# One output transfer for a tile with rows of two batches, and a store issued by ScalarE

## The chip, the cores and the metric

The kernel runs on one core of one Trainium2 chip. The metric is the device time of one execution in microseconds; a kernel's time is the median of several executions. A core has a matrix engine (TensorE, "PE" in the profile), VectorE (DVE), ScalarE (ACT), GpSimd (POOL), SyncE (SP, which here issues nearly all transfers), and 16 DMA engines that move the data between the chip's memory (DRAM) and the core's on-chip memory (SBUF, 128 partitions).

## The reference

Attention with a few extra "beacon" keys, and behind it a gated feed-forward layer:

```python
B, H, S, Nb, D = (8, 8, 576, 16, 64)
k_all = np.concatenate([beacon_k, k], axis=2)      # v_all likewise
scores = scale * np.matmul(q, k_all.transpose(0, 1, 3, 2))
scores = np.where(causal, -1000000000.0, scores)   # beacon keys are always seen
a = np.exp(scores - scores.max(-1, keepdims=True))
a /= a.sum(-1, keepdims=True) + 1e-09
x = np.matmul(a, v_all).transpose(0, 2, 1, 3).reshape(4608, 512)
out = (np.maximum(x @ w_gate, 0.0) * (x @ w_val)) @ w_out    # d_ff = 1536
```

The result has 4608 rows (8 batches of 576) of 512 float32.

## The kernel before, in words

The work is a list of tasks. Each task has the engines that may run it, a cost, the tasks it depends on, the buffers it holds and a priority. A planner (`Plan.order`) goes through them once on the host: it always takes the task that can begin first by its own estimates (then the one with the lowest priority number), and so writes one order of instructions for each engine. On the chip each engine works through its own list in that order and waits with semaphores. A transfer is a task of the queue "DMA", which is SyncE's list; its cost has two parts, the time to issue and the time on the wire.

For every batch, q, k and v are loaded into staging tiles `st` (lines 534, 614, 615, 617 and others), cast on GpSimd (line 500 into `h`, line 456 for v), turned by TensorE against the identity (line 511) and copied to their places. Scores are matmuls of lines 675 to 683, the exponential is line 709 on ScalarE, the division by the sum line 730 on GpSimd. The scaled weights `pb` are transposed by DMA (line 776) for all batches but the first, and line 786 multiplies them with v. The result lands transposed in `xT`.

The feed-forward layer works on 512 of a batch's 576 rows at a time (`REG` = 512): `hidden` makes the gate and value products (line 853), the ReLU (857) and their product `hT` (861). `project` then multiplies 128 rows of `hT` with `w_out` in three groups of four matmuls (line 873), copies the result from the accumulator into an output tile `osb` (`copy`, line 452 on ScalarE or 454 on VectorE) and stores it (line 885). There are four `osb` tiles, each 128 rows of 512 float32.

The last 64 rows of each batch are left over. They are gathered from four batches at a time, so that `hidden` sees 256 rows, and `project` sees two tiles of 128 rows, each with 64 rows of one batch and 64 rows of the next. Those two blocks of a tile lie 576 rows apart in the output, and the kernel stores them with one transfer for each. This happens twice: for batches 0 to 3 in the middle of the run, for batches 4 to 7 at its very end. The very last tile (`last` is true) is projected in two halves of 256 columns (`LAST_PARTS` = 2), so that the first half can be copied and stored while the second is still being multiplied.

The store's priority (`OUT` = -1300) puts it ahead of the loads that could begin at the same moment. A buffer is given back once all its users are done, which is the `users` count of `Hold`.

Of the kernel before, what the change touches and what calls it, by code (L numbers as in the profile page):

```python
# [55 lines left out]
OUT = -1300.0  # L56
# [93 lines left out]
class Plan:  # L150
# [7 lines left out]
    def add(self, engines, cost, run, deps=(), holds=(), prio=0.0, lag=None, part=0, lazy=0.0, after=0.0, move=0.0):  # L158
        t = Task(engines if isinstance(engines, tuple) else (engines,), cost, run, deps, holds, prio, lag, part, lazy, move)
        t.ready = after  # L160
        for d in t.deps:
            d.users.append(t)
        self.tasks.append(t)
        return t
# [112 lines left out]
def kernel(  # L277
# [12 lines left out]
    nc = tc.nc  # L290
    B, H, S, D = q.shape
# [4 lines left out]
    P = 128  # L296
# [54 lines left out]
    osb_s = outs  # L351
# [7 lines left out]
    f_s, v_ps, first_ps = Share(banks, F_MOST), Share(banks, V_MOST), Share(banks, FIRST_MOST)  # L359
# [3 lines left out]
    add = plan.add  # L363


    def c_dve(n):
        return 0.07 + 0.00104 * n
# [7 lines left out]
    def c_act(n):  # L375
        return 0.06 + 0.00083 * n
# [4 lines left out]
    def c_pe(n):  # L381
        return 0.002 + n / 2400.0
# [67 lines left out]
    def copy(e, dst, src):  # L450
        if e == "ACT":
            nc.scalar.copy(dst, src)  # L452
        elif e == "DVE":
            nc.vector.tensor_copy(dst, src)  # L454
        else:
            nc.gpsimd.tensor_scalar(dst, src, 1.0, 1.0, ALU.mult, ALU.mult)
# [408 lines left out]
    def project(t0, rows, here, hT, prio, last):  # L865
        w = DM // LAST_PARTS if last else DM
        for n0 in range(0, DM, w):
            ps, osb = Hold(f_s, 4), Hold(osb_s, 1 + len(rows))
            prev = None
            for part in range(3):  # L870
                def outp(_, part=part, ps=ps, n0=n0):
                    for nf in range(4 * part, 4 * part + 4):
                        nc.tensor.matmul(ps.tile[:, :w], hT[nf].tile[:, t0:t0 + P], wo_r[:, nf, n0:n0 + w],  # L873
                                         start=(nf == 0), stop=(nf == NF - 1))

                need = [prev, weight_in["o", part]]
                for hid in here:
                    need += hid[4 * part:4 * part + 4] + (hid[:11] if part == 0 else [])
                prev = add("PE", 4 * c_pe(w), outp, need, (ps,) + tuple(hT[4 * part:4 * part + 4]),
                           prio + 0.3 + 0.01 * part + 0.001 * (n0 > 0) - (0.5 if part else 0))  # L880
            ev = add(("ACT", "DVE"), {"ACT": c_act(w), "DVE": c_dve(w)}, lambda x, ps=ps, osb=osb: copy(
                x.engine, osb.tile[:, :w], ps.tile[:, :w]), (prev,), (ps, osb), -1000 + prio)
            at = 0
            for r0, n in rows:
                add("DMA", (0.4, 0.78 * n / P), lambda _, osb=osb, r0=r0, n=n, at=at, n0=n0: nc.sync.dma_start(
                    out[r0:r0 + n, n0:n0 + w], osb.tile[at:at + n, :w]), (ev,), (osb,), prio + OUT)
                at += n


    T0 = 10.0  # L890
# [15 lines left out]
    REG = S // MT * MT  # L906
    for b in range(B):
        hT = [Hold(hid_s, len(CUTS.get(b, ())) + 1 + REG // P) for _ in range(NF)]
        cuts = [0, *CUTS.get(b, ()), REG]
        prio = 1000 + 10.0 * b  # L910
        here = []
        for a, z in zip(cuts, cuts[1:]):
            here.append(hidden(lambda ki, a=a, z=z, b=b: xT[:, ki, b * S + a:b * S + z], z - a, a, done(b, a, z), hT, prio))
            for t0 in range(a // P * P, z // P * P, P):
                project(t0, [(b * S + t0, P)], [x for x, c0, c1 in zip(here, cuts, cuts[1:]) if c0 < t0 + P and c1 > t0],
                        hT, prio, False)
            prio += 2.0
    ends = xT.rearrange("p k (b s) -> p k b s", s=S)
    for i in range(2):
        b0, b1 = i * B // 2, (i + 1) * B // 2  # L920
        w = (b1 - b0) * (S - REG)
        prio = 1000 + 10.0 * b1 - 5.0
        hT = [Hold(hid_s, 1 + w // P + (LAST_PARTS - 1) * i) for _ in range(NF)]
        deps = [x for b in range(b0, b1) for x in done(b, REG, S)]
        hid = hidden(lambda ki, b0=b0, b1=b1: ends[:, ki, b0:b1, REG:], w, 0, deps, hT, prio)
        for t0 in range(0, w, P):
            b = b0 + t0 // (S - REG)
            project(t0, [(x * S + REG, S - REG) for x in (b, b + 1)], [hid], hT, prio, i == 1 and t0 + P == w)
# [37 lines left out]
```

## Time and profile before

| | |
|---|---|
| median of 3 runs | 411.87 us (411.68 to 412.15) |
| profiled execution | 410.77 us, of which the span is 408.7 us |
| TensorE busy | 394.9 us, 97% of the span |
| mean granted TensorE clock | 0.995 |
| output stores | 32 of 256 KB, 6 of 128 KB, 4 of 64 KB, all issued by SyncE at line 885 |
| median time from issue to landing | 2.4, 2.9 and 2.0 us for these three sizes |
| share of the chain that ended last | PE 87%, DMA 4%, POOL 3% |

An engine's row gives its busy time; the issuing of a transfer is not counted as busy, but has its own rows under "SPq". "Landing" is the moment at which a transfer's completion has arrived. A DMA share of 1 means that all 16 DMA engines have packets under way; overlapping packets can carry it over 1.

### The profile page before, as it was taken

The page shows a single profiled execution, that of the slowest core. Times are in us where ns is not written, and L with a number is a line of the kernel's source. Part 1 is how long each engine was busy: PE and PEld are TensorE (multiplying, and loading weights), DVE is VectorE, ACT ScalarE, POOL GpSimd, SP SyncE. Part 2 cuts the span into 40 slices and gives each one's busy share as a digit, 9 for nine tenths or more (in the row PEclk, how much of TensorE's full clock was granted, in tenths as well). Part 3 has the DMA queues.
Part 4 walks back from the last instruction along what each step waited for, and adds up shares of the span by engine and source line. Part 5 has one row for each costly group of instructions (what it writes and reads, how often), then busy time and mean ns, then how long its engine had stood idle before and what let it go on. Part 6 is the DMA issues. An engine that isn't in the chain of part 4 may idle for free.

```text
span 408.7 us, 10385 instructions
## 1 busy us (share of the span) xinstructions
PE 394.9 (97%) x3292; PEld 248.0 (61%) x3326; DVE 312.5 (76%) x1160; ACT 289.0 (71%) x958; POOL 234.5 (57%) x435
## 2 busy tenths in 40 slices
PE   8899999999999999999999999999999999999993
PEld 6667867587766868545557754555545544444482
DVE  7999899868999988889968988999877433244241
ACT  5998799769988987887977999978868133033030
POOL 5899697548985859487693877857818000000000
PEclk9999999999999999999999999999999999999997
DMA  8999999799899989999899999999492740200112
GB/s 201 194 236 211 211 174 159 143 267 239 193 218 179 235 182 232 192 223 220 193 213 217 225 196 218 199 182 243 108 199 53 169 71 0 95 9 2 53 51 51
DMA packets 172615, 68.02 MB, mean 166 GB/s; under 512 B 146832, under 2 KB 168080, under 8 KB 172560
## 3 DMA queue, kind: packets, MB, share of 16 engines
q1 hardware_dynamic: 167808, 62.64, 74.4%
q0 software_dynamic: 4752, 4.72, 7.2%
q8 instruction: 26, 0.43, 0.5%
q14 instruction: 29, 0.24, 0.2%
HBM read 38.27 MB, written 9.44 MB: 117 GB/s over the span
## 4 chain that ended last, share of the span: by engine, by line
PE 87%; DMA 4%; POOL 3%; DVE 2%; issue 1%; SPq 1%; ACT 1%; POOLq 0%; DVEq 0%; ACTq 0%
PE f L853 44%; PE f L873 23%; PE f L683 7%; PE f L786 6%; PE f L511 4%; DMA st<-in_q_dram 3%; PE f L675 2%; POOL xT L730 1%; DMA st<-in_v_dram 1%; PE f L815 1%; DVE f L698 1%; PE f L765 1%; PE f L678 1%; POOL h L500 1%; SPq L534 0%
## 5 line engine op out<-in xcount | busy, mean ns | idle before, releaser
L730 POOL TENSOR_SCALAR pb<-pb,small 128x448 bf16<-128x448 bf16 (+8 forms) x224 | 122.2, 560 | 56.1 <-DVE small L723 49.7
L709 ACT ACTIVATE pb<-f,small 128x64 bf16<-128x64 f32 (+7 forms) x256 | 131.8, 531 | 8.3 <-DVE small L698 3.4
L857 ACT ACTIVATE g<-f 128x512 f32<-128x512 f32 (+3 forms) x156 | 71.9, 475 | 66.5 <-PE f L853 54.0
L698 DVE CUSTOM_DVE_ANT_0 f<-f,mask 128x128 f32<-128x128 f32 (+7 forms) x256 | 112.2, 475 | 5.3 <-PE f L683 4.2
L853 PE MATMUL f<-xT,wv_r 128*128 128x512 bf16 (+3 forms) x618 | 110.6, 313 | 0.3
L853 PE MATMUL f<-xT,wg_r 128*128 128x512 bf16 (+3 forms) x616 | 109.2, 313 | 0.5
L861 DVE TENSOR_TENSOR hT<-g,f 128x512 bf16<-128x512 f32 (+3 forms) x156 | 79.9, 520 | 38.6 <-PE f L853 34.6
L873 PE MATMUL f<-wo_r,hT 128*128 128x512 bf16 (+1 forms) x425 | 100.8, 373 | 1.1 <-issue 0.2
L853 PEld LDWEIGHTS <-wg_r 128*128 128x128 bf16 x624 | 59.7, 98 | 32.0 <-issue 0.3
L853 PEld LDWEIGHTS <-wv_r 128*128 128x128 bf16 x624 | 58.8, 98 | 33.3 <-issue 0.7
L873 PEld LDWEIGHTS <-hT 128*128 128x128 bf16 x444 | 41.8, 98 | 40.7
L709 ACT ACTIVATION_READ_ACCUMULATOR pb<-f,small 128x1 f32 x256 | 55.9, 218 | 0.0
L683 PE MATMUL f<-kT,diag 128*128 128x128 bf16 (+7 forms) x256 | 46.0, 286 | 0.0
L698 DVE DVE_READ_ACCUMULATOR2_ANT small<- 128x1 f32 x296 | 41.2, 139 | 0.2
L500 POOL TENSOR_SCALAR h<-st 128x512 bf16<-128x512 f32 x62 | 37.8, 619 | 5.2 <-DMA st<-in_q_dram 1.8
L454 DVE COPY osb<-f 128x512 f32<-128x512 f32 (+1 forms) x24 | 16.3, 679 | 25.9 <-PE f L873 25.7
L511 PE MATMUL f<-ident,h 128*128 128x128 bf16 (+2 forms) x320 | 28.4, 216 | 3.5 <-POOL h L500 3.5
L730 POOL TENSOR_SCALAR xT<-xT,small 128x64 bf16<-128x64 bf16 (+2 forms) x64 | 27.2, 442 | 6.8 <-PE f L853 5.5
L454 DVE CAST diag<-f 64x512 bf16<-64x512 f32 (+2 forms) x54 | 28.7, 537 | 2.8 <-ACT diag L452 1.4
L511 PEld LDWEIGHTS <-h 128*128 128x128 bf16 (+2 forms) x320 | 21.0, 98 | 14.4 <-POOL h L500 5.8
L709 ACT ACTIVATE xT<-f,small 128x64 bf16<-128x64 f32 (+4 forms) x64 | 27.4, 448 | 2.6 <-issue 1.3
L695 DVE TENSOR_REDUCE small<-f 128x1 f32<-128x512 f32 x40 | 27.2, 679 | 1.9 <-PE f L675 1.0
(68 smaller groups left out, 367.6 us busy)
## 6 DMA issues: line engine op xcount, KB each, us to landing
st<-in_q_dram SPq DMA_DIRECT2D x32, 256.0 KB, 4.4
st<-in_k_dram SPq DMA_DIRECT2D x32, 256.0 KB, 4.6
out_dram<-osb SPq DMA_DIRECT2D x32, 256.0 KB, 2.4
st<-in_v_dram SPq DMA_DIRECT2D x24, 256.0 KB, 5.2
st<-in_v_dram SPq DMA_DIRECT2D x8, 224.0 KB, 4.5
wg_r<-in_moe_w_gate_dram POOLq DMA_DIRECT2D x3, 512.0 KB, 10.5
wv_r<-in_moe_w_val_dram POOLq DMA_DIRECT2D x3, 512.0 KB, 10.6
wo_r<-in_moe_w_out_dram POOLq DMA_DIRECT2D x3, 512.0 KB, 10.8
```

The costliest lines, as they stand in the source:

```text
L454: nc.vector.tensor_copy(dst, src)
L500: (nc.gpsimd if x.engine == "POOL" else nc.vector).tensor_scalar(to, of, by, 1.0, ALU.mult, ALU.mult)
L511: nc.tensor.matmul(to, h16.tile[:rows, a * P:(a + 1) * P], ident[:rows, :rows], start=True, stop=True)
L683: nc.tensor.matmul(view(i), t.diag.tile[:, p, j * P:j * P + P], kT[:, p, :n], start=True, stop=True)
L695: nc.vector.tensor_reduce(out=to, in_=view(i), axis=AX.X, op=ALU.min)
L698: nc.vector.tensor_tensor_reduce(out=view(i), in0=view(i), in1=msk, scale=1.0, scalar=small["t"][:, 0:1] if name in "EF" else 3.0e38, op0= ...
L709: nc.scalar.activation(ph.tile.rearrange("p a n -> p (a n)")[:, a:a + n], view(i), AF.Exp, bias=small["t"][:, low:low + 1], scale=-1.0, ac ...
L730: (nc.gpsimd if x.engine == "POOL" else nc.vector).tensor_scalar(one, one, small["t"][:, 8 + i:9 + i], 1.0, ALU.mult, ALU.mult)
L853: nc.tensor.matmul(to, w_r[:, ki, nf * P:(nf + 1) * P], x, start=(ki == 0), stop=(ki == KM - 1))
L857: r = add("ACT", c_act(w), lambda _, psg=psg, g=g: nc.scalar.activation(g.tile[:, :w], psg.tile[:, :w], AF.Relu), (a,), (psg, g), -1000 + ...
L861: hid.append(add("DVE", c_dve(w), lambda _, psv=psv, g=g, nf=nf: nc.vector.tensor_mul(hT[nf].tile[:, c0:c0 + w], g.tile[:, :w], psv.tile[: ...
L873: nc.tensor.matmul(ps.tile[:, :w], hT[nf].tile[:, t0:t0 + P], wo_r[:, nf, n0:n0 + w], start=(nf == 0), stop=(nf == NF - 1))
```

## The change

The blocks of rows of a tile are no longer stored one by one. For a tile of one batch the transfer is the same as before. For a tile with rows of two batches, the output is viewed as batch by row by column, and one transfer goes from the 128 partitions of `osb` to 2 batches x 64 rows (`REG:` to the end of the batch) x `w` columns. The output tile is held by two users, the copy and the store. For the first half of the very last tile, the copy is tied to ScalarE, and the store is a task of ScalarE with a cost of 0.6 us at the copy's priority: ScalarE issues it, not SyncE. All other stores stay with SyncE. The planner's cost of a store is 0.4 us to issue and 0.78 us on the wire; before, each block had 0.4 us and its share of 0.78.

```diff
     def project(t0, rows, here, hT, prio, last):
         w = DM // LAST_PARTS if last else DM
         for n0 in range(0, DM, w):
-            ps, osb = Hold(f_s, 4), Hold(osb_s, 1 + len(rows))
+            ps, osb = Hold(f_s, 4), Hold(osb_s, 2)
...
             ev = add(("ACT", "DVE"), {"ACT": c_act(w), "DVE": c_dve(w)}, lambda x, ps=ps, osb=osb: copy(
                 x.engine, osb.tile[:, :w], ps.tile[:, :w]), (prev,), (ps, osb), -1000 + prio)
-            at = 0
-            for r0, n in rows:
-                add("DMA", (0.4, 0.78 * n / P), lambda _, osb=osb, r0=r0, n=n, at=at, n0=n0: nc.sync.dma_start(
-                    out[r0:r0 + n, n0:n0 + w], osb.tile[at:at + n, :w]), (ev,), (osb,), prio + OUT)
-                at += n
+            if last and n0 == 0:
+                ev.engines, ev.cost = ("ACT",), {"ACT": c_act(w)}
+            to = out[rows[0][0]:rows[0][0] + P, n0:n0 + w] if len(rows) == 1 else out.rearrange("(b s) d -> b s d", s=S)[
+                rows[0][0] // S:rows[0][0] // S + len(rows), REG:, n0:n0 + w]
+            if last and n0 == 0:
+                add("ACT", 0.6, lambda _, osb=osb, to=to: nc.scalar.dma_start(to, osb.tile[:, :w]), (ev,), (osb,), -1000 + prio)
+                continue
+            add("DMA", (0.4, 0.78), lambda _, osb=osb, to=to: nc.sync.dma_start(to, osb.tile[:, :w]), (ev,), (osb,), prio + OUT)
```

## The prediction

> **What bounds the kernel now.** I read the page first (busy times and slices), then the chain of work that ended last for the final 30 us, then the timeline and the transfers of the output for the last 7 us, and last the stretch around 240 us where the first stores of two-batch tiles stand.
>
> The busy times and the table of 10 us stretches say that TensorE sets the pace: it has 97% of the span, and 9.89 to 9.95 us of each 10 us around the middle stores.
>
> ```profile
> PE 394.9 (97%) x3292; PEld 248.0 (61%) x3326; DVE 312.5 (76%) x1160; ACT 289.0 (71%) x958; POOL 234.5 (57%) x435
> ...
> 240.00:250.00 10.00, 9.89 (x53) 4.93 (x53) 9.23 (x40) 9.61 (x34) 6.01 (x12) 1.00 0.93 184
> ```
>
> The reader is to see that only two places are open to this change: the tail after the last matmul, and any stall that it puts into TensorE's row of work. The chain and the instruction queue of SyncE show the tail (start, length in us, what):
>
> ```profile
> 397.40 4.96 PE f L873 x34
> 402.36 0.02 issue
> 402.38 0.42 DVE osb L454
> ...
> 402.23 3.70 SPq L885 DMA_DIRECT2D out_dram<-osb  x6
> ...
> L885 SPq DMA_DIRECT2D out_dram<-osb x2: 546/566/587, 404.7 to 405.3; - x2
> ...
> DMA to landing us min/median/max: 2.0/2.0/2.1
> ...
> L961 SPq EVENT_SEMAPHORE  x11: 17/28/28, 406.0 to 408.7; - x11
> ```
>
> The last matmul ends at 402.34, the last copy at 402.80, but SyncE hands out six stores one behind the other from 402.23 to 405.93. The last of them, issued at about 405.34, lands 2.0 to 2.1 us later, near 407.4, and the closing waits end the span at 408.7. So 402.8 to 407.4 is spent on stores alone, some 2.5 us of it because the last store is sixth in the queue.
>
> What a store costs the 16 DMA engines is in two tables of stretches (the last two columns: busy share of the engines, GB/s). The first is a whole 128-row store behind TensorE's work, the others are the 64-row stores of the tail:
>
> ```profile
> 383.00:383.90 0.90, 0.90 (x5) 0.39 (x4) 0.07 (x1) 0.00 (x0) 0.00 (x0) 1.00 0.79 291
> ...
> 403.30:404.00 0.70, 0.00 (x0) 0.00 (x0) 0.00 (x0) 0.00 (x0) 0.00 (x0) 1.00 0.85 178
> 404.00:404.60 0.60, 0.00 (x0) 0.00 (x0) 0.00 (x0) 0.00 (x0) 0.00 (x0) 0.80 0.98 212
> ```
>
> A whole store moves 256 KB in 0.9 us at 291 GB/s with 0.79 of 16 engines busy: 291 / 16 / 0.79 = 23.0 GB/s for one busy engine. A store from 64 of the 128 partitions has the same 2 KB rows but only 178 to 212 GB/s, with the engines as busy.
>
> Last, the middle, in SyncE's queue, then GpSimd's and TensorE's rows for what the loads behind the stores feed:
>
> ```profile
> 239.29 3.52 SPq L885 DMA_DIRECT2D out_dram<-osb  x4
> 242.87 0.58 SPq L614 DMA_DIRECT2D st<-in_beacon_v_dram  x1
> 243.49 0.44 SPq L615 DMA_DIRECT2D st<-in_v_dram  x1
> 243.97 0.56 SPq L534 DMA_DIRECT2D st<-in_q_dram  x1
> ...
> DMA to landing us min/median/max: 3.8/3.8/3.8
> ...
> 248.59 0.62 POOL L500 TENSOR_SCALAR h<-st 128x512 bf16<-128x512 f32 x1
> ...
> 251.11 0.39 PE L511 MATMUL f<-ident,h 128*128 128x128 bf16 x4
> ```
>
> Four 64-row stores go out ahead of the loads of the next batch. The q load issued at 243.97 lands 3.8 us later at 247.8, is cast at 248.59 to 249.21 and turned by TensorE at 251.11: slack of 0.8 us before the cast and 1.9 us behind it, 2.7 us in all.
>
> **The change part by part.** (1) Ten 64-row stores become five 128-row ones: two in place of four at 239 us, three in place of six at the tail. (2) The store of the last tile's first half moves from SyncE to ScalarE's queue. (3) The copy of that half is tied to ScalarE, which made it already (0.37 us from 401.94): nothing. (4) The planner sees one issue of 0.4 us in place of two and the same 0.78 us of transfer, and the output buffer counts two users. Its loads may be handed out up to 0.4 us earlier; what follows could come in another order. A gain is bounded by TensorE's idle time in those stretches, 0.05 to 0.16 us in each 10 us, about 1 us to the end; a loss I bound by the same 1 us. I take 0.
>
> Issue time. At the tail SyncE issues two stores in place of six; the whole stores above took 0.33 us to issue, the 64-row ones 0.51 to 0.59. The last copy ends at 402.80 and SyncE is free by then (402.23 + 0.59), so the last store is issued at 402.85 instead of 405.34: 2.5 us sooner. ScalarE issues its store at about 402.35, right behind its copy, with only the closing drain queued behind it. The trace shows no issue by ScalarE; by SyncE's rows it is 0.33 to 1.59 us (the longest in the middle, with its queue full), beside the last copy, so 0 on the path.
>
> How the rows of a store are dealt to the engines decides the rest. Each hardware-queue load or store of the trace has a count of rows as its outermost count, 128, 112, 80, 64, 48 or 16; 16 divides them all, and each transfer ends with 16 small completion writes in the packet records. The q and k loads have a count of two as well, but inside the 128. The new stores are the first with a two outside: their DRAM side is 2 batches of 64 rows, 576 rows apart, while the SBUF side is 128 partitions. The trace cannot show whether they are dealt by rows (16 engines) or by the outermost count (2 engines), so both ends stand.
>
> The cheap end, 16 engines: whole stores as in the 291 GB/s row, 0.9 us for the first and 0.45 us for each half, landing at about 405.1 (402.85 + 2.0 to 2.4). 405.1 - 407.4 = -2.3 us, and the middle gains nothing, as TensorE has no wait there.
>
> The dear end, 2 engines: 2 x 23.0 = 46 GB/s. The tail's 512 KB take 11.4 us. The first data come 0.9 us after an issue (a whole store issued at 382.24 began to move near 383.1), so 403.1 + 11.4 = 414.5, and 0.4 us to the landing, as now: 414.9 against 407.4 is +7.5 us. All three stores use the same two engines, so ScalarE's queue saves nothing. In the middle the two stores also hold 512 KB: from 240.2 to 251.6 on these two engines, where the data of the four stores now end near 244.2 (fourth landing 244.6, less 0.4). Every load behind them has a sixteenth of its rows on each of these engines and so ends 7.4 us late; 2.7 us are slack, then GpSimd's cast waits, and TensorE stands still for 4.7 us at line 511. Bounds here: 0, if buffers and the order of work absorb it; and the whole 7.4 us plus as much again, if the 128x512 transposes by DMA (4.3 us to issue at 245.28) queue up too, 14 us.
>
> I take 2 engines. The nearest rows are the 64-row stores: they show that work is cut by position beforehand and not shared out, since engines freed of half the partitions brought no speed; and one cut by the outermost count fits every transfer of the trace without exception. The sum: -0 for issue (hidden behind the data), +7.5 at the tail, +4.7 in the middle: +12.2 us. The profiled execution took 410.77 us (span 408.7 and 2.07 around it): 423.0. It lies 1.1 us under the median of 411.87, so for the median: 424.1.
>
> The Trainium skill, page "DMA: Bandwidth & Descriptors", section "Rules for kernel authors", states that an outermost dimension of size c below 16 confines the whole transfer to at most c engines; by it the sum is the dear end, and no run here shows it yet. It speaks against this change; the same section also advises one transfer of 128 partitions in place of two from disjoint halves, which speaks for it, and by which alone the sum would be the cheap end.
>
> **The rivals.** (a) Dealt by rows, the cheap end: 411.87 - 2.3 = 409.6 us, faster. For it: the SBUF side still counts 128 and whole stores run at 291 GB/s. Against: the two blocks are not one run in DRAM. The point from which it decides: data must end by 407.0 to break even, 3.9 us for 512 KB, so 134 GB/s or 5.8 engines; with six or more engines the change gains, with fewer it loses. (b) Two engines, but the middle hidden: 411.87 + 7.5 = 419.4 us. For it: transposes by DMA land 9 us before use in that stretch (landing at 252, used at 261.5). Against: the 2.7 us of slack at the q load. (c) Two engines at the 64-row rate of some 12 GB/s each: twice the data times, +18.9 at the tail and 18.8 - 2.7 = 16 in the middle, about 447 us. Against: 24 GB/s in total is far under the 178 GB/s that half the partitions gave. (d) No difference: six engines, or a new queue's start cost on ScalarE that eats the 2.3 us: 411.9.
>
> **How the numbers follow.** Chances: forecast 0.62, (a) 0.13, (b) 0.20, (c) 0.02, (d) 0.03. A difference of 0.2% (0.8 us) is about what a measurement of this kernel can tell. Slower is 0.62 + 0.20 + 0.02 = 0.84, same 0.03, faster 0.13. Predicted 424 us. The range takes the forecast and (b) with their bounds: the low end is (b) with the three last stores on three different pairs of engines, where the longest, 256 KB at 46 GB/s, takes 5.7 us and lands at 409.2, +1.8, so 414; the high end is the forecast with the middle at 14 us, 433. It leaves out (a), (c) and (d), 0.18. The forecast's own range is 420 to 433.
>
> **What would show it.** In the profile after: three output stores at the tail, the last issued near 402.85 plus what the middle cost, landing some 12 us later, with a DMA share near 0.12 and about 46 GB/s in those stretches. In the middle: two stores landing 6 and 12 us after their issue, loads behind them 7 us late, and TensorE waiting 4 to 5 us for the casts of line 500. Landings 2.0 to 2.4 us after the issue and 291 GB/s would mean (a), and the prediction would be wrong in its step on dealing; an unbroken TensorE near 250 us would mean (b).

## The result, and the profile after

The changed kernel takes 426.72 us (median of 4 runs, 426.35 to 428.14) against 412.01 us before (4 runs of the same session): 3.6% slower, ratio 1.0364 with a 95% interval of 1.0339 to 1.0389. The forecast was 424 us, range 414 to 433. The profiled execution of the changed kernel took 428.14 us, of which the span is 426.4; it began about 1.5 us later than the one of before (the first matmul of line 853 stands at 34.8 us and not at 33.3, long ahead of anything that was changed), so positions below are compared with that in mind. This start moves between 32.6 and 35.2 us over all the profiled runs of this study.

The page of the changed kernel, its first lines and the slices of the DMA engines:

```profile
span 426.4 us, 10384 instructions
...
PE 397.8 (93%) x3290; PEld 249.0 (58%) x3326; DVE 312.1 (73%) x1156; ACT 288.3 (68%) x962; POOL 233.5 (55%) x435
...
DMA  8999998999999999999999749989866400101101
...
q10 hardware_dynamic: 130, 0.13, 0.1%
```

TensorE's share falls from 97% to 93%, while its busy time hardly moves (394.9 to 397.8 us): the time is waiting. The new queue q10 is ScalarE's; it carries 128 rows and two completion writes, 130 packets, where a transfer over 16 engines ends with 16.

The tail, first the chain that ended last, then the timeline, and then a table of stretches (last columns: granted TensorE clock, share of the 16 DMA engines, GB/s):

```profile
406.84 4.96 PE f L873 x34
411.80 0.02 issue
411.82 0.42 DVE osb L454
```

```profile
411.66 1.20 SPq L890 DMA_DIRECT2D out_dram<-osb  x2
411.78 1.30 ACTq L888 DMA_DIRECT2D out_dram<-osb  x1
```

```profile
413.50:414.50 1.00, 0.00 (x0) 0.00 (x0) 0.00 (x0) 0.00 (x0) 0.00 (x0) 1.00 0.13 20
414.50:416.50 2.00, 0.00 (x0) 0.00 (x0) 0.00 (x0) 0.00 (x0) 0.00 (x0) 0.70 0.13 39
416.50:418.50 2.00, 0.00 (x0) 0.00 (x0) 0.00 (x0) 0.00 (x0) 0.00 (x0) 0.50 0.13 51
```

The issues did what the change says: the last store is handed out at 412.35, 0.6 us after the last matmul, and not 3.0 us after it. Yet from the last matmul to the end of the span pass 14.6 us (411.8 to 426.4), where 6.4 us passed before. The share of 0.13 is two engines of 16 (2 / 16 = 0.125). They begin slowly, with 20 GB/s, and move about 50 GB/s from 416.5 us on.

The middle, in TensorE's timeline and waits, and GpSimd's timeline:

```profile
251.20 0.57 PE L683 MATMUL f<-kT,diag 128*128 128x448 bf16 x2
257.32 0.61 PE L511 MATMUL f<-ident,h 128*128 128x128 bf16 x4 [5.56 <-POOL h L500]
257.73 3.62 PE L853 MATMUL f<-xT,wv_r 128*128 128x512 bf16 x8
```

```profile
PE f L511 <- POOL h L500: 5.6, 1, 5.6
```

```profile
255.15 0.62 POOL L456 TENSOR_SCALAR v<-st 128x512 bf16<-128x512 f32 x1 [5.77 <-DMA st<-in_v_dram]
256.65 0.62 POOL L500 TENSOR_SCALAR h<-st 128x512 bf16<-128x512 f32 x1 [0.88 <-DMA st<-in_q_dram]
```

TensorE stands still for 5.56 us at the turn of line 511. It waits for GpSimd's cast, and GpSimd has waited 5.77 us for the v load and 0.88 us for the q load that stand behind the two stores. This is the only wait of TensorE after 235 us that the table of waits lists. A last table shows what follows the wait:

```profile
249.00:251.00 2.00, 1.95 (x11) 0.95 (x11) 2.00 (x12) 1.81 (x7) 0.38 (x1) 1.00 0.13 51
...
253.00:255.00 2.00, 0.00 (x0) 0.00 (x0) 0.00 (x0) 0.58 (x3) 0.00 (x0) 0.96 0.40 102
255.00:257.00 2.00, 0.00 (x0) 0.00 (x0) 0.00 (x0) 0.00 (x0) 0.97 (x2) 0.50 0.66 144
257.00:259.00 2.00, 1.68 (x7) 0.86 (x8) 0.68 (x1) 0.24 (x1) 1.69 (x4) 0.50 1.23 160
259.00:261.00 2.00, 2.00 (x6) 0.76 (x5) 1.25 (x3) 1.06 (x3) 1.45 (x4) 0.50 1.11 251
261.00:263.00 2.00, 2.00 (x10) 0.88 (x9) 1.72 (x7) 1.00 (x3) 1.89 (x5) 0.83 0.82 204
```

Before the wait the stores hold two engines at 51 GB/s again. During it the granted clock falls to 0.50, and it stays there until about 261.7, 4.4 us after TensorE has begun again. Eight matmuls of line 853 take 3.62 us in that state; at full clock eight of them take 1.89 us in both traces.

### The profile page after: what moved, and what is told of

It is laid out like the page before. It is cut to its first block, busy times and chain, and to the rows that moved or that the text cites. A ratio compares the mean times of both kernels' runs of the same rounds, so it can differ in the third digit from the quotient of the medians.

```text
span 426.4 us, 10384 instructions
## 1 busy us (share of the span) xinstructions
PE 397.8 (93%) x3290; PEld 249.0 (58%) x3326; DVE 312.1 (73%) x1156; ACT 288.3 (68%) x962; POOL 233.5 (55%) x435
## 4 chain that ended last, share of the span: by engine, by line
PE 80%; DMA 9%; POOL 3%; SPq 2%; DVE 2%; issue 1%; ACT 1%; POOLq 0%; DVEq 0%
PE f L853 40%; PE f L873 21%; PE f L683 6%; PE f L786 5%; DMA st<-in_v_dram 5%; PE f L511 4%; DMA st<-in_q_dram 2%; PE f L675 2%; POOL xT L730 1%; DMA st<-in_k_dram 1%; POOL h L500 1%; PE f L815 1%; DVE f L698 1%; SPq L614 1%; PE f L678 1%
## 5 line engine op out<-in xcount | busy, mean ns | idle before, releaser
L853 PE MATMUL f<-xT,wv_r 128*128 128x512 bf16 (+3 forms) x618 | 112.7, 316 | 0.3
L456 POOL TENSOR_SCALAR v<-st 128x512 bf16<-128x512 f32 (+1 forms) x39 | 24.0, 616 | 11.8 <-DMA st<-in_v_dram 11.8
```

What stands on the lines that cost most here:

```text
L853: nc.tensor.matmul(to, w_r[:, ki, nf * P:(nf + 1) * P], x, start=(ki == 0), stop=(ki == KM - 1))
```

## The experiments

Two causes lay close together, the stores themselves and the planner's new order, in which TensorE's instructions differ from about 250 us on. The first four runs take them apart. All ratios are against the kernel before in the same session; the range behind a ratio is its 95% interval.

**Only the middle.** The loop of before, with its two tasks, so that the order is the old one; the first task stores both blocks, the second nothing, for the tiles of batches 0 to 3.

```diff
+            whole = len(rows) == 2 and rows[0][0] < NT // 2
...
+                    if not whole:
+                        nc.sync.dma_start(out[r0:r0 + n, n0:n0 + w], osb.tile[at:at + n, :w])
+                    elif at == 0:
+                        nc.sync.dma_start(out.rearrange("(b s) d -> b s d", s=S)[r0 // S:r0 // S + 2, REG:, n0:n0 + w],
+                                          osb.tile[:, :w])
```

> The order of the work is that of before; only the two tiles near 239 us go out with one transfer each (2 batches x 64 rows), the tail keeps its six stores. Theory (a transfer is dealt to as many engines as its outermost count, here two): the two stores land 6 and 12 us or more after their issue, the loads behind them end some 8 us late, TensorE waits 4 to 6 us for the cast of line 500 and runs slower for a few us after it: 418 to 419.5 us. Rival (the loss in the middle comes from the planner's new order, not from the transfers): within 1 us of before, 411 to 413.

Measured: 419.4 us against 412.19, ratio 1.0187 (1.0155 to 1.0219). Its timeline of TensorE:

```profile
257.56 0.49 PE L511 MATMUL f<-ident,h 128*128 128x128 bf16 x4 [4.75 <-POOL h L500]
257.85 1.91 PE L853 MATMUL f<-xT,wv_r 128*128 128x512 bf16 x4
```

The wait is there with the old order. Four matmuls then take 1.91 us and not 1.03, the slow clock once more. From its first line-853 matmul to its last matmul of all, TensorE takes 375.6 us against 369.0 before, +6.6: 4.8 of waiting, and nearly all the rest is the clock. The rival for the middle falls.

**Only the tail.** The same loop with the condition `rows[0][0] >= NT // 2`; SyncE issues all three stores.

> The order of the work is that of before; only the three stores of the last two tiles are one transfer each, all issued by SyncE. Theory (two engines): from the last matmul to the end 14.6 us as in the changed kernel, in place of 6.4 us: 420.1 us, and a DMA share of 0.13 in those stretches. Rival (the slow tail comes from ScalarE's queue, which is used for the first time there): with SyncE alone the tail lands some 2 us earlier than before, 409.6 us.

Measured: 420.92 us, ratio 1.0222 (1.0188 to 1.0257). From the last matmul to the end 14.4 us, with ScalarE's queue unused. Two of its stretches:

```profile
407.00:410.00 3.00, 0.00 (x0) 0.00 (x0) 0.00 (x0) 0.00 (x0) 0.00 (x0) 1.00 0.13 37
410.00:414.00 4.00, 0.00 (x0) 0.00 (x0) 0.00 (x0) 0.00 (x0) 0.00 (x0) 0.50 0.13 50
```

The two parts cost 7.2 and 8.7 us, 15.9 in all, each known to some 1.4 us by its interval. The whole change cost 14.7 us in its own session, and 15.4 in this one with SyncE alone (the next run). So the two parts account for it.

**The changed kernel with SyncE alone.** `nc.scalar.dma_start` becomes `nc.sync.dma_start` in the store of the first half.

> The changed kernel with one thing altered: SyncE, not ScalarE, issues the store of the last tile's first half, at the same place in the order. Theory (three stores share two engines, so who issues them is hidden): 426.7 us, within 0.5. Rival (ScalarE's queue costs or saves by itself): off by more than 1 us.

Measured: 427.62 us, ratio 1.0388 (1.0357 to 1.0418), beside 1.0364 for the changed kernel in its own session. The difference of some 0.9 us in the medians is inside the limit set for the rival, but over the 0.5 us of the theory. The intervals of the two ratios overlap, and from the last matmul to the end it is 14.5 us against 14.6, so no effect of ScalarE's queue is shown.

**Rows that alternate.** The product `hT` is written with the rows of two batches alternating, and the output is viewed as row, batch, column. So the outermost count is 64, and the same 128 blocks of 2 KB (or 1 KB) go out.

```diff
-            to = out[rows[0][0]:rows[0][0] + P, n0:n0 + w] if len(rows) == 1 else out.rearrange("(b s) d -> b s d", s=S)[
-                rows[0][0] // S:rows[0][0] // S + len(rows), REG:, n0:n0 + w]
+            to = out[rows[0][0]:rows[0][0] + P, n0:n0 + w] if len(rows) == 1 else out.rearrange("(b s) d -> s b d", s=S)[
+                REG:, rows[0][0] // S:rows[0][0] // S + len(rows), n0:n0 + w]
...
+                    to = to.rearrange("p (t s b) -> p t b s", b=2, s=S - REG)
+                    x, y = [z.rearrange("p (t b s) -> p t b s", b=2, s=S - REG) for z in (x, y)]
+                nc.vector.tensor_mul(to, x, y)
```

> The changed kernel, but the rows of the two batches alternate on the partitions (the product hT is written in that order), so that the output side of the transfer counts 64 rows outside and 2 batches inside: the same bytes, rows and blocks, the same number of transfers and the same queues. Theory (dealt by the outermost count): 16 engines again, no wait near 250 us, the last store lands 2.0 to 2.4 us after its issue: 409.6 us, give or take 1 for the planner's new order. Rival (two blocks far apart in one transfer are slow as such): 420 us or more, as the changed kernel.

Measured: 409.79 us, ratio 0.9944 (0.9922 to 0.9967). Its transfers, and two stretches of the tail:

```profile
DMA to landing us min/median/max: 2.4/2.5/2.7
```

```profile
405.00:406.00 1.00, 0.00 (x0) 0.00 (x0) 0.00 (x0) 0.00 (x0) 0.00 (x0) 1.00 0.90 325
406.00:406.80 0.80, 0.00 (x0) 0.00 (x0) 0.00 (x0) 0.00 (x0) 0.00 (x0) 1.00 0.76 250
```

In the transfer nothing but the order of the two counts is turned round, and the stores run at 325 GB/s over 0.90 of the engines; TensorE has no wait after 230 us, and the end comes 4.25 us after the last matmul. So neither the two distant blocks nor one transfer for a tile is slow: the count that stands outside is. The price is on VectorE, whose products with alternating rows take 443 ns and not 421.

**Other counts.** Four whole-tile stores, hidden under TensorE, with other counts outside:

```diff
+            count = {6 * S: 8, 6 * S + 2 * P: 2, 7 * S: 4, 7 * S + 2 * P: 16}.get(rows[0][0])
...
+                    if count:
+                        to = to.rearrange("(r a) d -> a r d", a=count)
```

> The kernel before, with four whole-tile stores near the end laid out as (count outside, rows inside): 8 x 16 rows near 350 us, 2 x 64 near 355, 4 x 32 near 382, 16 x 8 near 387. The rows of these four tiles go to permuted places of the output; nothing else is altered, and TensorE hides all four, so the time stays at 412. Theory (as many engines as the outermost count, each at 23 GB/s, on top of the 2.0 us that a store takes from issue to landing with 16 engines, of which 0.7 are data): 8 land after 2.7 us, 4 after 4.1, 2 after 6.9, 16 after 2.0. Rival (an outer count below 16 falls to two engines, or one, whatever it is): 8 and 4 land like 2, after 6.9 us or more.

Here the outer count steps from one row of the output to the next, not over 576 rows. Each of these stores is followed by an ordinary whole store some 0.9 us later, which uses all 16 engines and so must wait for the busy ones. The profile has no landing of its own for a store with fewer than 16 completion writes, so the expected landings of counts 8, 4 and 2 cannot be read off; the store with count 16 landed after 2.9 us, not 2.0. The rows for the followers of counts 8, 2, 4 and 16, in this order:

```profile
DMA to landing us min/median/max: 4.0/4.0/4.0
```

```profile
DMA to landing us min/median/max: 7.8/7.8/7.8
```

```profile
DMA to landing us min/median/max: 5.4/5.4/5.4
```

```profile
DMA to landing us min/median/max: 2.7/2.7/2.7
```

Counted from the issue of the special store, its follower lands after 3.5, 4.9, 6.3 and 8.7 us for counts 16, 8, 4 and 2. With 128 / count + 8 rows on the busiest engine (16, 24, 40 and 72), at 2 KB / 23 GB/s = 0.089 us for a row, the steps should be 0.7, 1.4 and 2.8 us; they are 1.4, 1.4 and 2.4. So the delay grows with each halving of the count and does not jump to the worst at once, and a count of 2 is the slowest with neighbouring rows too; the first step is the poorest fit. The completion records agree without a time: the semaphores of the stores with counts 8, 4 and 2 have 457, 453 and 451 records, where a full set has 464. That is 7, 11 and 13 fewer, as it must be if 8, 4 and 2 engines each write one and the issuer one more in place of 16. The time stayed (410.3 us, one run).

**The new order alone.** The planner sees the changed kernel's tasks, but every 64-row block is stored by a transfer of its own (first with ScalarE for the first half, then with SyncE alone).

```diff
+            def store(queue, osb=osb, n0=n0):
+                at = 0
+                for r0, n in rows:
+                    queue.dma_start(out[r0:r0 + n, n0:n0 + w], osb.tile[at:at + n, :w])
+                    at += n
```

> The planner sees what it sees in the changed kernel, and so writes the same new order, but every block of 64 rows is stored by a transfer of its own: four by SyncE near 240 us, at the tail two by SyncE, two by ScalarE, two by SyncE. Theory (the loss is all in the dealing of the new transfers; the new order costs less than 1 us; at the tail the last issue comes 1.2 us sooner, but 512 KB at the 178 to 212 GB/s of 64-row stores take 2.6 us, so the end gains about 1.0): 411.2 us, give or take 1. Rival (the new order loses some us by itself): 413 or more.

Measured: 409.67 us, ratio 0.9957 (0.994 to 0.9973), a little faster than the kernel before and 0.5 us under the theory's range: 5.1 us from the last matmul to the end, 1.3 us less than before.

> The planner's new order as in the changed kernel, every block of 64 rows stored by a transfer of its own, and SyncE issues all of them: the new order and nothing else. In the traces so far kernels in the new order have 1.7 us around their span and those in the old order 2.05. Theory (the gain of the run with the new order and 64-row stores is 1.3 us from ScalarE's two issues at the tail and 0.35 us from around the span, and the order is worth nothing inside the span): 0.35 us faster than before, 411.3 us, with 6.35 us from the last matmul to the end. Rival (the new order saves TensorE time): 410.3 or less.

Measured: 412.28 us, ratio 1.0004 (0.999 to 1.0018). No worth of the new order is shown: the rival's gain is excluded, and the 0.35 us of the theory lies within the interval (0.6 us to each side), so it is neither shown nor excluded. The time around the span is 1.7 us again and not 2.05.

**ScalarE's queue alone.** The old order and 64-row stores; only the queue of two stores is altered.

```diff
+                queue = nc.scalar if last and n0 == 0 else nc.sync
```

> The kernel before with one thing altered: ScalarE issues the two 64-row stores of the last tile's first half. Theory (the last issue comes 1.2 us sooner, and 5.05 us pass from the last matmul to the end, not 6.35): 1.3 us faster than before, 410.3 us. Rival (the engines, not the issues, set the end of the tail): within 0.4 us of before.

Measured: 410.36 us, ratio 0.9964 (0.995 to 0.9977). The second part of the change, by itself and with 64-row stores, is a gain of 1.6 us (0.9 to 2.1). Of these, 1.3 us stand at the tail, where 5.1 us pass from the last matmul to the end and not 6.4. The timeline shows why: SyncE's issues take 2.4 us in all, where they took 3.7.

```profile
402.80 2.43 SPq L886 DMA_DIRECT2D out_dram<-osb  x4
402.92 1.32 ACTq L886 DMA_DIRECT2D out_dram<-osb  x2
```

**Alternating rows without ScalarE, in either order.**

> The kernel with alternating rows, with SyncE in place of ScalarE for the store of the last tile's first half. Theory (with 16 engines the issue is on the path again: one more issue of 0.55 to 0.6 us ahead of the last store): 0.6 us slower than with ScalarE, 410.4 us. Rival (the last store waits for the engines, not for its issue): no difference, 409.8.

> Alternating rows and one transfer for a tile, all issued by SyncE, but the order of work of the kernel before (the planner still sees two stores). Against the run with SyncE and the new order it shows what the new order is worth. Theory (nothing): 410.4 us, within 0.6. Rival (the old order was the better one): 409 or less.

Measured: 409.2 us (0.9938, 0.9916 to 0.996) and 409.96 us (0.9964, 0.9948 to 0.9981). With alternating rows it is no loss to leave ScalarE out. The last issue then comes 1.20 us after the last matmul and not 0.56, but the last landing 3.29 and not 3.10: this fits the rival, by which the engines set the end. The old order is not better either. The three kernels with alternating rows beat the kernel before by 0.4 to 0.6%; their intervals overlap, so no order among them is shown.

## Why the prediction was right

The forecast was right in its cause, its sign and, within 3 us, its size. One term was missing, TensorE's clock, and the path by which the loads came late was only in part the one described.

*How the rows are dealt.* The dear end was the right one. The step rested on one fact, that 16 divides every outermost count of the trace, and on a reading of the 64-row stores; neither was proof. That reading took engines to be free while those stores ran, but the share in the same rows is 0.85 to 0.98: all were busy, so the rows say nothing of how work is dealt. The run with alternating rows shows the step, since in the transfer it alters the order of the counts alone, and the run with other counts shows the grading. The Trainium skill, page "DMA: Bandwidth & Descriptors", section "Rules for kernel authors", had said that an outermost dimension below 16 confines a transfer to at most that many engines. Here the runs agree with it: a share of 0.13 for a count of two, and completion records that fit 8, 4 and 2 engines.

*The tail.* Forecast +7.5 us, measured +8.2 (14.6 against 6.4 us from the last matmul to the end). The 11.4 us of data at 46 GB/s were 12.0 in the packet records (412.87 to 424.91): the rate reached 50 GB/s, but the first 3 us ran below it, and what slowed them was not tried. The first data also came 1.2 us after the first issue and not 0.9. That ScalarE's issue would save nothing was right: the three stores shared one pair of engines (the share stays at 0.12 to 0.14 from 413.5 to 425 us).

*The middle.* The loads were to end 7.4 us late. Measured from the first of the stores, the q load lands 15.9 us later (240.53 to 256.47) where it took 8.4 (239.29 to 247.73): 7.5 us late. Less 2.7 us of slack gives 4.8 us, against 4.7 in the forecast; with the old order the wait is 4.75 us. In the changed kernel it is 5.56, because the new order brings the turn four matmuls earlier. That the size fits so well is in part luck. The two stores landed 8.0 and 12.1 us after their issue, where 6 and 12 were forecast, and the loads were held in two ways, not one. SyncE itself was held: issuing the q load took 4.27 us and not 0.56.

```profile
246.24 4.27 SPq L534 DMA_DIRECT2D st<-in_q_dram  x1
```

So 14 of its 16 completion writes, at 252.5 to 253.3, are late as well, and the last two come at 255.8 and 256.5. In the run with the middle alone ten of the 16 come last, at 256.6 to 256.7. How the delay divides between held issues and busy engines is not shown.

The term that was missing is the clock: about 2 us. The eight matmuls behind the wait took 1.7 us longer than at full clock, and the turn ahead of them and the scores behind share the rest. Rival (b), a hidden middle, is excluded by the same wait, and rival (c), 24 GB/s, by the 50 GB/s. The high end of the range should have been 434: twice 7.4 is 14.8, not 14.

*The planner's order* was put at 0, with 1 us to each side; the run with nothing but the new order gives 1.0004 (0.999 to 1.0018).

*Rival (a)*, 16 engines, was priced at 409.6 us with a chance of 0.13. The kernel that does get 16 engines runs in 409.79. The price of the gain was right and it was there to be had; but the reason for it was only half right, since the 2.5 us of earlier issue were to bring 2.3, and without ScalarE's part of them the time is the same.

*The sum.* In the two profiled executions the span grows by 17.7 us: 1.5 at the start, 5.6 of waiting, about 2.2 of slow clock (4.4 us at half speed), 0.2 left over in the rest of TensorE's row, 8.2 at the tail. The medians differ by 14.7; the start, which moves from run to run, and 0.3 us less around the span make up for most of the difference, and about 1 us stays with the scatter of single executions.

## What to carry to other kernels

Before two transfers are merged into one, look at which count then stands outside on either side. A merged transfer with 2 outside and 64 inside ran on two engines at 50 GB/s, the same blocks with 64 outside on 16 engines at 325 GB/s. A DMA share that stays at a round fraction (0.13 here) while nothing else is busy is the mark of it in a profile, and the loads queued behind such a store pay as well. And where a chain of issues on one queue sets the end of a kernel, a second queue alone brought 1.6 us; with whole-tile stores over 16 engines it brought nothing that shows.

## What the runs showed of the hardware that was not expected

A wait of TensorE cost more than its length, and how much more depended on when the clock changed. In the changed kernel TensorE stops at 251.76; the granted clock is 0.96 in the stretch from 253 to 255 and 0.50 from 255 on, so it fell at about 254.8, some 3 us after the stop, and it came back at 261.7, 4.4 us after the new start. That adds about 2 us to a wait of 5.56. In the run with the middle alone TensorE stops at 252.81 and begins again at 257.56:

```profile
255.00:260.00 5.00, 2.44 (x10) 1.06 (x11) 0.20 (x1) 1.86 (x5) 3.73 (x8) 0.77 0.86 191
260.00:265.00 5.00, 5.00 (x26) 2.35 (x25) 3.06 (x14) 3.32 (x10) 2.27 (x5) 0.89 1.31 226
```

Clocks of 0.77 and 0.89 mean 2.3 and 1.1 us at half speed, that is from about 257.7 to 261.1. So the clock fell 4.9 us after the stop, when TensorE was already at work again, and the wait of 4.75 us still cost about 1.7 us more. At the end of the kernel the fall comes 2.0 us after the last matmul before the change (from the clock of 0.80 in the prediction's row from 404.0 to 404.6), and 5.1 us after it with the tail alone. In the clock records of all twelve traces every stretch between two changes is a whole multiple of 3.413 us; the two slow ones here last 6.83 and 3.41. The Trainium skill, page "TensorE: Matmul & The Clock Gate", section "Part 1: The HAM clock gate (the "warmup" mystery)", gives about 3.4 us of idleness for the fall and as much busy time for the return; the step of 3.413 us agrees, the delays are wider here: 2.0 to 5.1 us for the fall, 3.6 and 4.4 for the return. Waits of at most 0.8 us, between 30 and 235 us of both profiled executions, left the clock at full; what waits between 0.8 and 4.75 us cost no run here shows.

The 2-batch stores of 128 rows took 0.58 to 0.68 us to issue as the first of their group, and still 0.59 us with alternating rows, where whole stores of one batch take 0.33 in quiet stretches; the forecast had put 0.33 to 0.59 there, and it cost nothing, since SyncE was free again just as the last copy ended (412.24). Kernels in the new order have 1.7 us around their span and those in the old order 2.05, in each of their runs; what makes that difference was not tried.
